# Low parts of x and of two weight groups summed by TensorE and copied out by ScalarE, in a gated linear attention with a feed-forward block

## The chip, the cores and the metric

The kernel runs on one core of a Trainium2 chip. The metric is the device time of one execution in microseconds. The kernel before took 530.58, 530.69 and 531.53 us in three runs; the median is 530.69 us.

In what follows PE is TensorE, DVE is VectorE, ACT is ScalarE, POOL is GpSimd and SP is the engine that only issues the transfers (DMA).

## The reference

A gated linear attention over 4 batches, 8 heads, 768 tokens and 48 elements a head feeds a two-layer feed-forward block:

```python
for t in range(S):
    state = alpha[:, :, t, :, None] * state + np.einsum('bhd,bhe->bhde', k[:, :, t], v[:, :, t])
    y[:, :, t] = np.einsum('bhd,bhde->bhe', q[:, :, t], state)
x = np.ascontiguousarray(y.transpose(0, 2, 1, 3)).reshape(B * S, H * D)   # 3072 x 384
h = x @ w_in                       # 384 x 2048
g = np.maximum(0.01 * h, h)
out = (g @ w_out).astype(np.float32)
```

q, k, v and alpha are float32. Both weight matrices are float32 values times a float64 scalar, so they arrive as float64, as pairs of 32-bit words, and the kernel takes the words apart itself.

## The kernel before, in words

**Precision.** The feed-forward products are done in fp32r, the faster and shorter form of float32 on PE. To keep float32's precision each operand is held as a high part (the value rounded to fp32r) and a low part (the value minus the high part, rounded too), and each product is the sum of three: high by high, high by low and low by high. The low parts are what the change is about. For x (the attention's output) they are made in `outputs`: ACT copies the sum y out of PSUM as the high part (L418), and DVE subtracts that from y into the low part (L419). For the weights they are made in `converting`, once for each of the 16 groups f of 128 hidden elements: ACT scales the upper words (L245), DVE builds a float32 `bits` from them (L248, L251), ACT rounds it to the high part (L254), DVE takes a power of two from it (L258), subtracts the high part (L260), scales the lower words by that power into `pw` (L262), and adds the two into the low part (L265).

**Attention.** A unit is 128 tokens of one batch, all 8 heads; there are 24, and three make a block of 384 tokens for the feed-forward part. For the first nine units (`u < AHEAD`) alpha, q and k are loaded token by token and transposed by PE (L280); for the others DVE transposes them. DVE makes the running product of alpha (L314) and a reversed one (L320) and scales q and k with them (L339, L347). PE then computes the scores of even heads from rows 0 to 47 and of odd heads from rows 64 to 111 of its array, into two PSUM tiles (L356), ACT copies them out (L366), POOL masks them (L367), PE transposes the scaled k back (L380), multiplies the old state by q (L395, from the fifth unit on), adds scores by v (L401) and computes the update of the state (L412). ACT sums absolute values of the two running products for a range check (L332).

**Feed-forward.** `ffn_in` runs nine matmuls of 384 columns for one block and one group f (L493), then ACT, DVE, ACT and DVE in turn make the activated high part `gh` (L496, L499, L501) and low part `gl` (L505); `ffn_out` runs nine matmuls into the three output tiles (L520), three steps later. Blocks 0 and 1 go together, group by group, while the weights are still being converted; the other six follow one by one with the attention of units 9 to 23 woven in.

**What sets the order.** The program is written in one order and a scheduler that estimates times orders the instructions of each engine anew, so a change of a few instructions can move others. Each engine then runs its own list strictly in that order. The conversions of groups 0, 1 and 2 are started while the attention of units 6 to 8 is done; those of later groups are held between the steps of blocks 0 and 1 by explicit lists (`put`).

**PSUM.** There are eight banks: two for `ph` (the feed-forward's first product), and three each of two kinds, `a` and `b`, that the attention takes in turn, eight of them a unit. The sum y of a unit lies in a bank of kind b for the first eight units and of kind a for the ninth.

**SP's queue.** All loads go through SP in one order: alpha, q, k and v of the first nine units, then the weight groups. v has three places, so v of unit u+3 is asked for once the outputs of unit u are done.

Of the kernel before, what the change touches and what calls it, by code (L numbers as in the profile page):

```python
# [9 lines left out]
F32 = mybir.dt.float32  # L10
F32R = mybir.dt.float32r
I32 = mybir.dt.int32
U32 = mybir.dt.uint32
I64 = mybir.dt.int64
AF = mybir.ActivationFunctionType
ALU = mybir.AluOpType
# [6 lines left out]
def gated_linear_attn_ffn(ctx, tc, q, k, v, alpha, w_in, w_out, out):  # L23
    nc = tc.nc
    B, H, S, D = q.shape
    NT, DM = out.shape
    DF = w_in.shape[1]
    P = 128
# [7 lines left out]
    BR = HB + D  # L36
# [12 lines left out]
    ps_h = fast.enter_context(tc.tile_pool(name="ps_h", bufs=2, space=bass.MemoryType.PSUM))  # L49
# [7 lines left out]
    PITCH = RUN + GAP  # L57
    AHEAD = 3 * UPB
    LAG = 3
    SOON, EARLY = 2, 3  # L60
    LEAD = 8
    SL = 8 * UPB
# [10 lines left out]
    def pieces(name, dtype, *shapes):  # L73

        sizes = [math.prod(shape) for shape in shapes]
        whole = cst.tile([P, sum(sizes)], dtype, name=name)
        parts = []
        for n, shape in enumerate(shapes):
            part = whole[:, sum(sizes[:n]):sum(sizes[:n + 1])]
            axes = "abc"[:len(shape)]  # L80
            if len(shape) > 1:
                part = part.rearrange(f"p ({' '.join(axes)}) -> p {' '.join(axes)}", **dict(zip(axes, shape)))
            parts.append(part)
        return parts
# [4 lines left out]
    state, vals_sb, rest = rest[:B], rest[B:B + NV], rest[B + NV:]  # L89
    loads_sb = [[rest.pop(0) for _ in range(n)] for n in NL]  # L90

    spare = pieces("spare", F32, *[(NP * PITCH,)] * 3)
    x_sb, = pieces("large", F32R, (3 * (NG + 1), 2, TB))

    w_sb = {}
# [8 lines left out]
    made = {}  # L104
# [75 lines left out]

    keep_warm(6)
    make_identity(nc, ident)
    nc.gpsimd.memset(mask, 1.0)
    nc.gpsimd.affine_select(
        out=mask, in_=mask, compare_op=ALU.is_ge, fill=0.0, base=0,
# [31 lines left out]
    def put(ordered, eng, op, *args):  # L217

        if not ordered:
            return op(*args)  # L220
        line = lines[eng]
        with tc.issue_after(line[-1].ins) if line else nullcontext():
            line.append(op(*args))
        return line[-1]

    def converting(f, ordered=False):

        if f >= NF:
            return
        raw = jobs.pop(f)  # L230
        w_sb[f] = cst.tile([P, 2, 2 * DM], F32R, name=f"w{f}")
        hi, lo = w_sb[f][:, HIGH, :], w_sb[f][:, LOW, :]
        if not f64:
            val = raw[:, :, 0:P].bitcast(F32)
            hi, lo = (t.rearrange("p (g f) -> p g f", f=P) for t in (hi, lo))
            nc.scalar.copy(hi, val)
            made["w", f] = nc.vector.tensor_tensor(lo, val, hi.bitcast(F32), ALU.subtract)
            return
        words = raw.rearrange("p g (f w) -> p (g f) w", w=2)
        top, low = words[:, :, 1], words[:, :, 0]  # L240
        bits = cvp.tile([P, 2 * DM], I32, name="bits", bufs=NBITS)
        val = bits.bitcast(F32)

        with nullcontext() if lines["ACT"] else behind(*AFTER.get(f, ("hi", f - 1))):
            put(ordered, "ACT", lambda: nc.scalar.mul(top.bitcast(F32), top.bitcast(F32), 2.0 ** -112))  # L245
        yield
        with nullcontext() if lines["ACT"] else behind("w", f - 1):
            put(ordered, "DVE", lambda: nc.vector.tensor_scalar(  # L248
                bits, top, 3, 0x7FFFFFF8, ALU.logical_shift_left, ALU.bitwise_and))
        yield  # L250
        put(ordered, "DVE", lambda: nc.vector.scalar_tensor_tensor(  # L251
            bits, top, -0x80000000, bits, ALU.bitwise_and, ALU.bitwise_or))
        yield
        made["hi", f] = put(ordered, "ACT", lambda: nc.scalar.copy(hi, val))  # L254
        yield
        pw = cvp.tile([P, 2 * DM], I32, name="pw", bufs=NPW)
        rest = pw.bitcast(F32)
        put(ordered, "DVE", lambda: nc.vector.tensor_scalar(pw, bits, -0x800000, None, ALU.bitwise_and))  # L258
        yield
        put(ordered, "DVE", lambda: nc.vector.tensor_tensor(val, val, hi.bitcast(F32), ALU.subtract))  # L260
        yield
        put(ordered, "DVE", lambda: nc.vector.scalar_tensor_tensor(  # L262
            rest, low.bitcast(U32), 2.0 ** -52, rest, ALU.mult, ALU.mult))
        yield
        made["w", f] = put(ordered, "DVE", lambda: nc.vector.tensor_tensor(lo, rest, val, ALU.add))  # L265
# [119 lines left out]
    def outputs(u):  # L385
        tb, b = units[u]
        i, j = divmod(u, UPB)
        pe, qs, ktok = live[u][:3]
        V, W = vals_sb[u % NV], state[b]
        at = i % 3 * (NG + 1)  # L390
        y = banks4()

        if tb:
            for p in range(NP):
                nc.tensor.matmul(  # L395
                    y[0:BR, p, :], W[0:BR, p, :], qs[0:BR, p, :], start=p == 0, stop=False, skip_group_check=True
                )
        for p in range(NP):
            for s, lo, m in ((0, 0, D if tb else HB), (1, HB, D)):
                c = (2 * p + s) * D  # L400
                nc.tensor.matmul(  # L401
                    y[lo:lo + m, p, :], V[:, c:c + m], masked[u][s][:, p, :],
                    start=not tb and p == 0, stop=p == NP - 1, skip_group_check=True,
                )
        del masked[u]
        kv = None
        if tb < NC - 1:
            kv = bank()[:, 0:NP * D].rearrange("d (p e) -> d p e", p=NP)
            for p in range(NP):
                for s, lo, m in ((0, 0, HB), (1, HB, D)):  # L410
                    h = 2 * p + s
                    made["kv", u] = nc.tensor.matmul(  # L412
                        kv[lo:lo + m, p, :], ktok[:, p, lo:lo + m], V[:, h * D:(h + 1) * D], start=True, stop=True
                    )
        load_values(u + NV)
        live[u] = pe, kv
        xh, xl = (x_sb[0:BR, at:at + NP, n, j * C:(j + 1) * C] for n in (0, 1))
        made["xh", u] = nc.scalar.copy(xh, y[0:BR])  # L418
        made["x", u] = nc.vector.tensor_tensor(xl, y[0:BR], xh.bitcast(F32), ALU.subtract)  # L419

    def next_state(u):
        tb, b = units[u]
# [61 lines left out]
    def ffn_in(i, f, steps=None):  # L484
# [14 lines left out]
        put(ordered, "DVE", lambda: nc.vector.tensor_tensor(t, ph, t, ALU.max))  # L499
        gh = ffp.tile([P, TB], F32R, name="gh", bufs=LAG + 1)  # L500
        put(ordered, "ACT", lambda: nc.scalar.copy(gh, t))  # L501
        for step in second:
            next(step, None)
        gl = ffp.tile([P, TB], F32R, name="gl", bufs=LAG + 1)
        made["gl", i, f] = put(ordered, "DVE", lambda: nc.vector.tensor_tensor(gl, t, gh.bitcast(F32), ALU.subtract))  # L505
# [48 lines left out]
    for n, _ in enumerate(st):  # L554
        if n == 2:
            load_values(NV - 1)
        while LOADS and LOADS[0][0] in made:
            key, f, part = LOADS.pop(0)
# [3 lines left out]
        u = AHEAD - EARLY + converted  # L562
# [4 lines left out]
        if n in STARTS:  # L567
            i, f = items[len(gs)][:2]
# [8 lines left out]
    for n in range(len(items) + LAG):  # L577
        slices = 0
        if n < len(items):
            i, f, slices, _ = items[n]  # L580
# [27 lines left out]
        for half in range(2):  # L608
# [5 lines left out]
            if half == 0 and n >= LAG:  # L614
                i, f, _, tag = items[n - LAG]
# [130 lines left out]
```

## Time and profile before

| | |
|---|---|
| median of 3 runs | 530.69 us |
| span of the profiled execution | 530.9 us |
| PE busy | 518.5 us (98%), 3778 matmul records |
| weight loads of PE busy | 500.0 us (94%) |
| DVE busy | 379.0 us (71%) |
| ACT busy | 230.7 us (43%) |
| POOL busy | 62.6 us (12%) |
| DMA | 46.64 MB |

The page shows no time around the span; the profiled execution's own time is taken as its span of 530.9 us, which lies within the three runs' 530.58 to 531.53.

Busy shares are means over unlike stages. The first 50 us or so are the attention of the first seven units, with all engines at work and the transfer engines full; then come two units more with the first feed-forward products, and from about 70 us on the feed-forward products alone, up to about 160 us. After that the rest of the attention and the feed-forward part run side by side. A float32 matmul shows as two records of PE, an fp32r matmul or a transpose as one.

### The profile page before, as it was taken

How to read it: one execution, taken by the hardware profiler on the slowest of the kernel's cores; microseconds unless marked ns; L12 is line 12 of the kernel's file. 1: busy time of each engine (PE TensorE's matmuls, PEld its weight loads, DVE VectorE, ACT ScalarE, POOL GpSimd, SP SyncE). 2: the span in 40 equal slices, each digit the busy share in tenths (PEclk: the TensorE clock that was granted, in tenths of full speed). 3: DMA queues.
4: the chain of work that ended last, by engine and by line, in shares of the span. 5: the costliest groups of instructions: out<-in, count | busy, mean ns of one | idle time of the engine just before them, and what ended most of it. 6: DMA issues, size and time to landing. Idle time of an engine off the chain costs nothing.

```text
span 530.9 us, 9962 instructions
## 1 busy us (share of the span) xinstructions
PE 518.5 (98%) x3778; PEld 500.0 (94%) x3778; DVE 379.0 (71%) x695; ACT 230.7 (43%) x489; POOL 62.6 (12%) x143
## 2 busy tenths in 40 slices
PE   8997999999999999999999999999999999999995
PEld 7886999999999999999999999999999999999995
DVE  6998899999999997777577586585786534333331
ACT  2764855555534444444334444345344444333331
POOL 4554500000000111100101101101010000000000
PEclk9998999999999999999999999999999999999998
DMA  9999975545726533552251431433201000101001
GB/s 144 168 175 170 229 172 133 131 122 141 170 45 184 127 84 81 102 134 49 60 111 30 112 83 44 92 74 86 54 15 25 31 16 1 23 1 44 1 0 51
DMA packets 92982, 46.64 MB, mean 88 GB/s; under 512 B 57856, under 2 KB 90112, under 8 KB 92928
## 3 DMA queue, kind: packets, MB, share of 16 engines
q1 hardware_dynamic: 92928, 45.93, 39.5%
q8 instruction: 32, 0.52, 0.4%
q14 instruction: 22, 0.18, 0.1%
HBM read 38.83 MB, written 4.72 MB: 82 GB/s over the span
## 4 chain that ended last, share of the span: by engine, by line
PE 87%; DVE 7%; DMA 4%; issue 1%; SPq 0%; DVEq 0%; ACT 0%
PE ph L493 35%; PE b L520 32%; PE a L356 4%; PE a L401 3%; PE a L520 3%; DMA small<-in_v_dram 3%; PE a L395 3%; PE a L412 2%; PE b L401 1%; PE a L380 1%; PE b L280 1%; DMA small<-in_alpha_dram 1%; DVE pw L262 1%; DVE gl L505 1%; DVE t L499 1%
## 5 line engine op out<-in xcount | busy, mean ns | idle before, releaser
L493 PE MATMUL ph<-large,w 128*128 128x384 f32 x1152 | 226.6, 338 | 0.5 <-DVE t L499 0.5
L493 PEld LDWEIGHTS ph<-large,w 128*128 128x128 f32 x1152 | 200.1, 188 | 2.8 <-DVE t L499 1.1
L520 PE MATMUL b<-w,gh 128*128 128x384 f32 x672 | 168.9, 340 | 0.0
L499 DVE TENSOR_TENSOR t<-ph,t 128x384 f32<-128x384 f32 x128 | 70.7, 553 | 79.1 <-ACT t L496 78.9
L520 PEld LDWEIGHTS b<-w,gh 128*128 128x128 f32 x672 | 119.4, 188 | 2.1 <-issue 0.4
L496 ACT ACTIVATE t<-ph 128x384 f32<-128x384 f32 x128 | 62.5, 489 | 128.2 <-PE ph L493 128.2
L501 ACT CAST gh<-t 128x384 fp32r<-128x384 f32 x128 | 65.7, 513 | 119.6 <-DVE t L499 119.6
L520 PE MATMUL b<-w,gl 128*128 128x384 f32 x336 | 107.4, 335 | 0.0
L505 DVE TENSOR_TENSOR gl<-t,gh 128x384 fp32r<-128x384 f32 x128 | 70.9, 554 | 34.3 <-ACT gh L501 34.2
L520 PEld LDWEIGHTS b<-w,gl 128*128 128x128 f32 x336 | 62.6, 188 | 0.0
L367 POOL TENSOR_SCALAR_AFFINE_SELECT sm<-sm 128x512 f32<-128x512 f32 x33 | 23.1, 712 | 207.8 <-ACT sm L366 207.8
L356 PEld LDWEIGHTS a<-qs,ks 48*128 48x128 f32 x312 | 24.1, 188 | 5.1 <-issue 4.2
L356 PE MATMUL a<-qs,ks 48*128 48x128 f32 x312 | 28.7, 285 | 0.0
L289 DVE STREAM_TRANSPOSE ks<-small 128x512 f32<-128x512 f32 x15 | 16.7, 1123 | 14.6 <-PE a L380 14.6
L324 POOL COPY pe<-pc 128x4 f32<-128x4 f32 x24 | 4.8, 202 | 163.7 <-DVE pc L314 163.7
L373 POOL TENSOR_TENSOR small<-us,pe 48x192 f32<-48x192 f32 x40 | 22.4, 560 | 1.5
L314 DVE TENSOR_TENSOR_SCAN pc<-e,small 128x128 f32<-128x128 f32 x60 | 20.4, 401 | 0.0
L366 ACT COPY sm<-a 128x512 f32<-128x512 f32 x24 | 14.0, 583 | 14.0 <-PE b L356 12.9
L520 PE MATMUL a<-w,gh 128*128 128x384 f32 x96 | 19.6, 337 | 0.0
L320 DVE TENSOR_TENSOR_SCAN rc<-e,small 128x511 f32<-128x511 f32 x15 | 19.1, 1276 | 0.2
L401 PE MATMUL a<-sm,small 128*48 128x128 f32 x256 | 17.7, 277 | 0.0
L254 ACT CAST w<-bits 128x768 fp32r<-128x768 f32 x16 | 13.4, 838 | 8.4 <-DVE bits L251 7.8
(92 smaller groups left out, 554.4 us busy)
## 6 DMA issues: line engine op xcount, KB each, us to landing
raw<-in_moe_w_out_dram SPq DMA_DIRECT2D x16, 384.0 KB, 3.8
small<-in_v_dram SPq DMA_DIRECT2D x24, 192.0 KB, 3.7
raw<-in_moe_w_in_dram SPq DMA_DIRECT2D x32, 144.0 KB, 4.0
out_dram<-o SPq DMA_DIRECT2D x24, 192.0 KB, 2.0
small<-in_alpha_dram SPq DMA_DIRECT2D x32, 96.0 KB, 2.3
small<-in_q_dram SPq DMA_DIRECT2D x30, 96.0 KB, 2.4
small<-in_k_dram SPq DMA_DIRECT2D x30, 96.0 KB, 2.2
small<-in_alpha_dram SPq DMA_DIRECT2D x30, 80.0 KB, 2.4
```

Of the source, the lines that this page charges most:

```text
L314: nc.vector.tensor_tensor_scan(pc[:, p, :], aT[:, p, :], ones.broadcast_to([P, C]), 1.0, ALU.mult, ALU.mult)
L320: nc.vector.tensor_tensor_scan(flat[2][:, NP * C - 2::-1], flat[0][:, NP * C - 1:0:-1], flat[1][:, NP * C - 2::-1], last, ALU.mult, ALU.add)
L356: nc.tensor.matmul(ss[s][:, p, :], ks[lo:lo + D, p, :], qs[lo:lo + D, p, :], start=True, stop=True)
L367: made["mask", u] = nc.gpsimd.affine_select(out=sm[s], in_=sm[s], compare_op=ALU.is_ge, fill=0.0, base=0, pattern=[[0, NP], [1, C]], chann ...
L373: nc.gpsimd.tensor_tensor(*scalings.pop(0))
L401: nc.tensor.matmul(y[lo:lo + m, p, :], V[:, c:c + m], masked[u][s][:, p, :], start=not tb and p == 0, stop=p == NP - 1, skip_group_check=True,
L493: nc.tensor.matmul(ph, w_in_of(f, wn, g), xt[:, g, :], start=n == 0, stop=n == 3 * NG - 1)
L496: put(ordered, "ACT", lambda: nc.scalar.mul(t, ph, 0.01))
L499: put(ordered, "DVE", lambda: nc.vector.tensor_tensor(t, ph, t, ALU.max))
L501: put(ordered, "ACT", lambda: nc.scalar.copy(gh, t))
L505: made["gl", i, f] = put(ordered, "DVE", lambda: nc.vector.tensor_tensor(gl, t, gh.bitcast(F32), ALU.subtract))
L520: product = nc.tensor.matmul(po[j], gt[:, js], w_out_of(f, wn), start=f == 0 and n == 0, stop=f == NF - 1 and n == 2)
```

## The change

For the first nine units the low part of x is no longer subtracted by DVE. PE adds the product of a negative identity (`minus`, made once by POOL) and the high part to the sum y where it lies in PSUM, which leaves y minus the high part there, and ACT copies that out. For weight groups 0 and 1 (`f < SUMS`) the last subtraction and the last addition on DVE are left out. PE sums identity by value, negative identity by high part and identity by scaled lower words in a PSUM tile of kind `ph`, for each half of 384 columns, and ACT copies the two sums out.

```diff
+    SUMS = 2
...
+    minus, = pieces("minus", F32R, (P,))
     x_sb, = pieces("large", F32R, (3 * (NG + 1), 2, TB))
...
     make_identity(nc, ident)
+    nc.gpsimd.tensor_scalar(minus, ident, -1.0, None, ALU.mult)
     nc.gpsimd.memset(mask, 1.0)
...
         put(ordered, "DVE", lambda: nc.vector.tensor_scalar(pw, bits, -0x800000, None, ALU.bitwise_and))
         yield
+        if f < SUMS:
+            nc.vector.scalar_tensor_tensor(rest, low.bitcast(U32), 2.0 ** -52, rest, ALU.mult, ALU.mult)
+            for cs in (slice(0, DM), slice(DM, 2 * DM)):
+                ps = ps_h.tile([P, 512], F32, name="ph")[:, 0:DM]
+                nc.tensor.matmul(ps, ident, val[:, cs], start=True, stop=False)
+                nc.tensor.matmul(ps, minus, hi[:, cs], start=False, stop=False)
+                nc.tensor.matmul(ps, ident, rest[:, cs], start=False, stop=True)
+                made["w", f] = nc.scalar.copy(lo[:, cs], ps)
+            return
         put(ordered, "DVE", lambda: nc.vector.tensor_tensor(val, val, hi.bitcast(F32), ALU.subtract))
...
         made["xh", u] = nc.scalar.copy(xh, y[0:BR])
-        made["x", u] = nc.vector.tensor_tensor(xl, y[0:BR], xh.bitcast(F32), ALU.subtract)
+        if u < AHEAD:
+            nc.tensor.matmul(y[0:BR], minus[0:BR, 0:BR], xh, start=False, stop=True, skip_group_check=True)
+            made["x", u] = nc.scalar.copy(xl, y[0:BR])
+        else:
+            made["x", u] = nc.vector.tensor_tensor(xl, y[0:BR], xh.bitcast(F32), ALU.subtract)
```

The new lines move the old ones by up to 16: L280 becomes L292, L356 L368, L366 L378, L380 L392, L395 L407, L401 L413, L412 L424, L418 L430, L332 L344. The new matmuls are L267, L268 and L269 (weights) and L432 (x); the new copies are L270 and L433.

The scheduler's order differs in the first 75 us or so; from the third weight group on, PE's list is the same as before. Three places:

PE, third unit (number 2), before, from its scores to its outputs. `a` and `b` are PSUM banks, `qs` and `ks` the scaled q and k, `ktok` (in later rows) the transposed k; `small` holds the loads and the identity.

```order
L356 MATMUL a_356<-qs_303,ks_311 128x128
L356 MATMUL b_357<-qs_303,ks_311 128x128
L356 MATMUL a_356<-qs_303,ks_311 128x128
L356 MATMUL b_357<-qs_303,ks_311 128x128
...
L380 MATMUL a_375<-small_73,ks_311 128x112 x4
L280 MATMUL a_392<-small_73 128x128 x4
L280 MATMUL b_384<-small_73 128x128 x4
L401 MATMUL b_400<-sm_366,small_73 64x128
```

The same place now; `b_316` is y of the unit before, `minus_75` the negative identity.

```order
L368 MATMUL a_360<-qs_306,ks_314 128x128 x4
L392 MATMUL a_379<-small_73,ks_314 128x112 x4
L368 MATMUL b_361<-qs_306,ks_314 128x128 x4
L292 MATMUL a_396<-small_73 128x128 x2
L432 MATMUL b_316<-large_76,minus_75 112x512
L292 MATMUL a_396<-small_73 128x128 x2
```

The eight score matmuls, which went to a and b in turn, are now four for a, then the transposes of k, then four for b. The same is so in units 4 and 6; in units 0, 1, 3, 5 and 7 they are in turn as before, and in unit 8 too, but for four of the sums that stand behind the first two. The sum for the unit before stands among the next transposes.

PE, seventh unit (number 6), where the sums for weight group 0 now stand (`ph_683` and `ph_688` are the two halves, `b_693` is y of unit 5). Before, L395 followed the transposes here directly.

```order
L368 MATMUL b_753<-qs_665,ks_672 128x128 x4
L432 MATMUL b_693<-large_76,minus_75 112x512
L292 MATMUL a_786<-small_73 128x128 x2
L267 MATMUL ph_683<-bits_675,small_73 128x384
L267 MATMUL ph_688<-bits_675,small_73 128x384
L268 MATMUL ph_683<-w0_674,minus_75 128x384
L268 MATMUL ph_688<-w0_674,minus_75 128x384
L424 MATMUL a_806<-small_73,ktok_775 64x48
...
L269 MATMUL ph_683<-pw_680,small_73 128x384
L269 MATMUL ph_688<-pw_680,small_73 128x384
L292 MATMUL b_779<-small_73 128x128 x4
L407 MATMUL b_793<-qs_665,small_73 112x128 x4
```

The update of the state (L424) moved ahead of the outputs (L407, L413), between the parts of the sums.

SP, around the seventh load of v (for unit 6), before:

```order
L139 DMA small_73<-in_q_dram 128x8x48
L449 DMA large_75<-large_75 16x3x768
L139 DMA spare_74<-in_alpha_dram 128x8x48
L449 DMA large_75<-large_75 16x3x768
L158 DMA small_73<-in_v_dram 128x8x48
L213 DMA raw_512<-in_moe_w_out_dram 128x384
```

And now:

```order
L141 DMA small_73<-in_q_dram 128x8x48
L465 DMA large_76<-large_76 16x3x768
L160 DMA small_73<-in_v_dram 128x8x48
L141 DMA spare_74<-in_alpha_dram 128x8x48
L216 DMA raw_518<-in_moe_w_out_dram 128x384
```

This load of v moved ahead of one load of alpha and of the second half of the first block's gather (`large` to `large`), which now comes after the second weight group.

## The prediction, on record before the change was run

> **What bounds the kernel now.** I read the page's busy shares first, then a table of stretches, then each engine's instructions in order of time through the stretch that the change touches. The shares are no answer by themselves:
>
> ```profile
> PE 518.5 (98%) x3778; PEld 500.0 (94%) x3778; DVE 379.0 (71%) x695; ACT 230.7 (43%) x489; POOL 62.6 (12%) x143
> ```
>
> The table by stretches has, for each: its length, the busy time of PE, of PE's weight loads, DVE, ACT and POOL, PE's granted clock, the share of the transfer engines and GB/s.
>
> ```profile
> 10.00:20.00 10.00, 9.93 (x130) 8.29 (x130) 9.71 (x23) 6.58 (x17) 4.41 (x11) 1.00 1.18 166
> 20.00:30.00 10.00, 9.67 (x132) 7.96 (x130) 9.44 (x21) 7.23 (x19) 6.29 (x15) 1.00 1.00 162
> 30.00:40.00 10.00, 9.88 (x122) 8.75 (x117) 9.05 (x20) 6.36 (x16) 5.21 (x13) 1.00 1.03 188
> 40.00:50.00 10.00, 6.55 (x78) 5.25 (x77) 9.52 (x18) 5.31 (x12) 6.08 (x8) 0.99 1.26 186
> 50.00:60.00 10.00, 10.00 (x119) 9.27 (x121) 8.47 (x17) 5.95 (x13) 3.22 (x6) 0.84 0.97 179
> 80.00:90.00 10.00, 10.00 (x59) 9.81 (x58) 10.00 (x18) 4.78 (x9) 0.00 (x0) 1.00 0.42 103
> ```
>
> From 10 to 50 us PE and DVE are both nearly full, so either might set the pace. What decides is who waits for whom. The scores (L356) need DVE's `qs`; the row of PE shows when they start, the row of DVE when `qs` was ready:
>
> ```profile
> 18.56 0.68 DVE L339 TENSOR_TENSOR qs<-b,pc 128x512 f32<-128x512 f32 x1
> ...
> 20.44 0.37 PE L356 MATMUL a<-qs,ks 48*128 48x128 f32 x1
> ```
>
> `qs` is done at 18.56 + 0.68 = 19.24, and PE comes to it 1.2 us later. Twice in this stretch it is DVE that waits for PE's transposes:
>
> ```profile
> 29.30 1.37 DVE L314 TENSOR_TENSOR_SCAN pc<-b,small 128x128 f32<-128x128 f32 x4 [0.20 <-PE b L280]
> ...
> 34.76 1.37 DVE L314 TENSOR_TENSOR_SCAN pc<-b,small 128x128 f32<-128x128 f32 x4 [0.53 <-PE b L280]
> ```
>
> So PE sets the pace, with one hole, in its rows between 44 and 53 us:
>
> ```profile
> 44.88 0.66 PE L280 MATMUL b<-small 128*128 128x128 f32 x4 [0.53 <-DVE rc L320]
> ...
> 46.56 0.63 PE L280 MATMUL b<-small,spare 128*128 128x128 f32 x4
> ...
> 49.98 0.42 PE L401 MATMUL b<-sm,small 128*48 128x128 f32 x1 [2.79 <-DMA small<-in_v_dram]
> ...
> 52.85 0.51 PE L356 MATMUL a<-qs,ks 48*128 48x128 f32 x1
> ```
>
> PE waits 2.79 us for v of unit 6, and after that its clock is 0.84 in the mean of the next ten microseconds. From 53 us on I find no idle time of PE up to the last block (the stretches of 50 and 80 us show it 10.00 busy of 10, and the rows of 81.26 and 82.86 below follow each other without a gap): whatever is added to PE there or before, beyond what this hole takes in, reaches the end.
>
> **The change part by part.** *Sums for x.* Nine matmuls of 512 columns in fp32r (L432). The nearest row is L493, 384 columns of the same type:
>
> ```profile
> 182.15 1.56 PE ph L493 x9
> ```
>
> That is 1.56 / 9 = 0.173 us each, so 0.173 × 512/384 = 0.231 at 512. Each stands between float32 transposes, and a change of shape and type costs PE a little: where the trace enters fp32r work from float32 work I find 0.08 us above the natural distance between starts; the nearest quoted row is the first score record, 0.37 against 0.27 for those that follow, 0.10. I take 0.231 + 0.084 = 0.315, nine times 2.8 us. Bounds: 9 × 0.231 = 2.1 with no entry, and 9 × 0.43 = 3.9 with twice 0.10.
>
> *Scores no longer in turn.* Today a score record of `a` and one of `b` start within 0.01 us of each other, since they use different rows of the array:
>
> ```profile
> 20.65 0.27 PE L356 MATMUL a<-qs,ks 48*128 48x128 f32 x1
> 20.66 0.27 PE L356 MATMUL b<-qs,ks 48*128 48x128 f32 x1
> 20.77 0.27 PE L356 MATMUL a<-qs,ks 48*128 48x128 f32 x1
> 20.77 0.27 PE L356 MATMUL b<-qs,ks 48*128 48x128 f32 x1
> ```
>
> A pair each 0.11 us, eight pairs a unit. Units 2, 4 and 6 now run four matmuls (eight records) of `a`, the transposes, and eight records of `b`: sixteen times 0.11 in place of eight, 8 × 0.107 to 0.11 = 0.87 us more. Three units: 2.6 us. Bounds: 0, if records of one row group are started as closely when the other is idle, and 3.3 with 0.2 for the shape changes of each.
>
> *Sums for two weight groups.* Each group has four float32 matmuls of 384 columns (L267, L269) and two in fp32r (L268). The nearest float32 row is L395, whose eight records are four matmuls of 128 columns:
>
> ```profile
> 39.05 0.88 PE b L395 x8
> ```
>
> 0.88 / 4 = 0.22 for 128 columns, 0.66 for 384. Four of these and two of 0.173 are 2.99 us a group, 6.0 for both; bounds 5.8 (0.107 a record, the closest spacing of score records) and 6.6 (0.1 for each of six changes of type). The trace shows float32 as two records of twice an fp32r record's length, four lengths in all: 0.66 against 0.173 is 3.8.
>
> [...]
>
> *Added to PE*: 2.8 + 2.6 + 6.0 = 11.4 us (bounds 7.9 to 13.8).
>
> *What the hole takes in.* v of unit 6 is asked for at 41.45 and lands at 49.84, after an alpha load and a gather half on SP's queue (the first three rows are SP's, the last is of the chain of waits):
>
> ```profile
> 40.08 0.55 SPq L139 DMA_DIRECT2D spare<-in_alpha_dram  x1
> 40.68 0.68 SPq L449 DMA_DIRECT2D large<-large  x1
> 41.45 0.54 SPq L158 DMA_DIRECT2D small<-in_v_dram  x1
> ...
> 41.45 8.39 DMA small<-in_v_dram
> ```
>
> In the change its issue moves ahead of those two, by about 1.3 us in the queue. It needs a place of v to come free at the outputs of unit 3, which PE reaches later by what is added to units 0 to 3 (three or four sums at 0.315 and one split, about 2 us), so I expect the landing between 49 and 51. PE comes to its first user later by the sums of units 0 to 5 (1.9), three splits (2.6) and group 0's first four matmuls and more (2 to 3): about 7 us of work after 46.56 + 0.6 = 47.2, less 0.8 of small idle times, so near 53. The wait is gone with 2 us to spare, and with it the slow clock: the rows above have 52.85 - 49.98 = 2.87 us from the first output to the next scores, where the unit before took
>
> ```profile
> 34.58 0.31 PE L401 MATMUL b<-sm,small 128*48 128x128 f32 x1
> ...
> 36.15 0.37 PE L356 MATMUL a<-qs,ks 48*128 48x128 f32 x1
> ```
>
> 1.57, 1.3 more; with the first score record at 0.51 for 0.37 that is 1.4. PE idles 10 - 6.55 = 3.45 in 40 to 50, and 0.3 in 20 to 30, on an earlier load of v. Together 3.45 + 1.4 + 0.3 = 5.15 us come back (bounds 3.3, the 2.79 and 0.53 alone, to 5.9, with the idle 0.7 that the stretches from 10 to 40 show beside).
>
> *DVE's relief.* It loses nine L419, and L260 and L265 twice:
>
> ```profile
> L419 DVE TENSOR_TENSOR large<-b,large 112x512 fp32r<-112x512 f32 x8 | 5.4, 673 | 0.8 <-ACT large L418 0.8
> L260 DVE TENSOR_TENSOR bits<-bits,w 128x768 f32<-128x768 f32 x9 | 9.0, 999 | 0.0
> L265 DVE TENSOR_TENSOR w<-pw,bits 128x768 fp32r<-128x768 f32 x9 | 8.6, 954 | 0.0
> ```
>
> 9 × 0.673 + 2 × (0.999 + 0.954) = 10.0 us. I cost it at nothing, since PE is late and not DVE. The one place where it may count is the stretch of steady feed-forward, where both are full:
>
> ```profile
> 81.26 1.60 PE ph L493 x9
> 82.86 1.58 PE a L520 x9
> ...
> 87.58 1.62 PE ph L493 x9
> ```
>
> 36 matmuls take 87.58 - 81.26 = 6.32 us, against 4 × 1.56 = 6.24 at PE's own rate: 0.08 a group, at most 0.9 us over the eleven groups to 150 us, and I count none of it. ACT's added copies (nine near 0.585, four near 0.515, 7.3 us) go to an engine that is half idle there; their price is only their place in the queue, which is a rival below. The one instruction on POOL is nothing beside its 4 to 6 us busy of 10.
>
> *Sum*: 11.4 - 5.15 = +6.2 on the profiled 530.9, so 537.1; that execution is 0.2 over the median, so **536.9 us**. Its own range, from the bounds: 7.9 - 5.9 = +2 to 13.8 - 3.3 = +10.5, 533 to 541.
>
> **The rivals.** *No change, about 531.* PE's busy time hides slack that the sums fill. For it: weight loads of PE are busy only 8.29 + 7.96 + 8.75 + 5.25 = 30.25 of the 40 us from 10 to 50, 9.75 us free, and with 1.4 of slow clock that is 11.2, nearly the 11.4 added: 530.9 + 0.2, 531. Against it: the score pairs' loads run side by side and the rows of PE follow each other at a constant distance, as in the rows of 20.65 to 20.77. [...] The wait of DVE for PE at 34.76 speaks against it. Chance 0.11.
>
> *Faster, about 526.* DVE, 95% busy, paces the first 50 us through a chain I have read wrongly, and 10 us less work on it pulls in all that follows. What it can win is capped by PE's idle time and slow clock, since PE has no gap after 53: 530.9 - 4.9 = 526, and it needs the sums to lie inside PE waits that the trace doesn't name. Against it: DVE's waits at 29.30 and 34.76. Chance 0.11.
>
> *Slower still, about 542.* The bank of y comes free later. Before, DVE's L419 frees it, in unit 1 at 22.31 + 0.67 = 22.98:
>
> ```profile
> 20.55 0.58 ACT L418 CAST large<-b 112x512 fp32r<-112x512 f32 x1 [0.44 <-PE b L401]
> ...
> 22.31 0.67 DVE L419 TENSOR_TENSOR large<-b,large 112x512 fp32r<-112x512 f32 x1
> ...
> 23.69 0.64 ACT L332 ACTIVATE rc<-rc 128x512 f32<-128x512 f32 x1
> ```
>
> Now ACT's second copy stands behind the next unit's score copies and sums of L332 in its queue, which ended at 24.33, so the bank can come 1.35 us later; there are three b banks and four uses a unit, and PE strictly in order waits with everything behind. Half of 1.35 in each of eight units is 5.4 above the forecast: 542. It decides if the copy ends after the next use of that bank is due. For it: PE is full, each wait counts. Against it: the sum itself stands early among the next transposes, and PE's own work per unit grows by more than 0.3. Chance 0.15.
>
> That the change doesn't do what it says can be left out: nine L419 and two of L260 and L265 are gone from DVE's list.
>
> **How the numbers follow.** Forecast 0.63, no change 0.11, faster 0.11, slower still 0.15. Such a measurement tells about 0.2% from no change, 1.1 us. Slower by more: the forecast less a little for its lower end, the last rival, and some of the no-change case that lies just beyond: 0.78; within: 0.10; faster: 0.12. The range leaves out the faster case and the top half of the last rival: 530.5 to 542.
>
> **What would show it.** No PE wait for v near 47 to 50 and a clock of 1.0 there; scores of units 2, 4, 6 at one record each 0.11 us; records of L267 and L269 at 0.33 spacing; the steady row of 81.26 about 6 us later, with period 6.3 unchanged. A b bank's wait on ACT's L433 ahead of L292 or L413 would speak for the last rival. If the steady row stands where it stood or earlier, the reading that PE sets the pace was wrong.

## The result, and the profile after

The changed kernel takes 539.15 us (median of four, 538.75 to 539.27); the kernel before, on the same chip, 531.11 us (530.58 to 532.03). The ratio is 1.015, interval 1.0135 to 1.0164: slower by about 8 us. Forecast were 536.9 us, in a range of 530.5 to 542, with a chance of 0.78 for slower.

The page of the changed kernel shows PE with 10 us more busy time and DVE with 9 us less:

```profile
PE 528.9 (98%) x3807; PEld 507.7 (94%) x3807; DVE 370.0 (69%) x682; ACT 238.1 (44%) x502; POOL 59.5 (11%) x144
```

The table by stretches (length, busy time of PE, weight loads, DVE, ACT, POOL; granted clock; share of the transfer engines; GB/s), for the changed kernel:

```profile
10.00:20.00 10.00, 9.80 (x131) 8.13 (x130) 8.69 (x19) 6.92 (x18) 4.43 (x11) 1.00 1.30 163
20.00:30.00 10.00, 10.00 (x102) 8.08 (x101) 7.81 (x17) 6.36 (x16) 4.73 (x12) 1.00 1.10 168
30.00:40.00 10.00, 10.00 (x117) 8.28 (x116) 6.78 (x16) 5.89 (x16) 4.73 (x11) 1.00 0.97 177
40.00:50.00 10.00, 10.00 (x99) 8.31 (x95) 8.86 (x18) 8.72 (x20) 4.96 (x10) 1.00 1.28 202
50.00:60.00 10.00, 9.58 (x88) 7.11 (x86) 6.34 (x14) 5.65 (x13) 3.61 (x8) 1.00 1.05 179
```

Against the same rows of before: the 6.55 of PE in 40 to 50 us is now 10.00, the clock of 0.84 in 50 to 60 is 1.00, and DVE has fallen from between 8.5 and 9.7 to between 6.3 and 8.9. The hole is full and its slow clock gone, as forecast; the 0.42 us that PE still idles in 50 to 60 us are a wait of L267 for DVE's `bits` in unit 7. PE's rows show what fills the hole. First unit 2, where `a` and `b` scores no longer start in pairs; then the stretch around the sums for weight group 0:

```profile
20.38 1.16 PE L368 MATMUL a<-qs,ks 48*128 48x128 f32 x8
21.47 0.60 PE L392 MATMUL a<-small,ks 112*128 112x112 f32 x4
22.00 1.16 PE L368 MATMUL b<-qs,ks 48*128 48x128 f32 x8
...
48.17 0.49 PE L432 MATMUL b<-large,minus 112*112 112x512 f32 x1
48.50 0.38 PE L292 MATMUL a<-small 128*128 128x128 f32 x2
48.73 1.45 PE L267 MATMUL ph<-bits,small 128*128 128x384 f32 x4
49.72 0.81 PE L268 MATMUL ph<-w,minus 128*128 128x384 f32 x2
50.46 0.67 PE L424 MATMUL a<-small,ktok 128*64 128x48 f32 x16
51.05 1.56 PE L269 MATMUL ph<-pw,small 128*128 128x384 f32 x4
```

Within each of the two pieces a row follows the last without idle time. In the chain of waits the row of steady feed-forward that stood at 81.26 now stands at

```profile
88.35 1.56 PE ph L509 x9
```

7.1 us later; its period has gone from 6.32 us to 6.26 (the next one is at 94.61).

The views of the cores give the span and the mean clock of a profile. Below are before, the changed kernel, and a second profile of before, taken beside the experiments (`before_again`):

```profile
core 0: 530.9 us, clock 0.994
```

```profile
core 0: 537.5 us, clock 0.999
```

```profile
core 0: 529.3 us, clock 0.997
```

The time of an execution is longer than its span, by 1.7 to 1.9 us in the runs here: 537.5 and 539.21 for the changed kernel, 529.3 and 530.99 for the second profile of before, 528.9 and 530.63 for another execution of it; 1.7 us in these three. So the first profile of before, with its span of 530.9, is an execution of about 532.6 us, some 1.5 to 2 us over the median. This is where the forecast went wrong, as shown below.

### The profile page after: what moved, and what is told of

Same layout as the page of the kernel before. It is cut to its first block, busy times and chain, and to the rows that moved or that the text cites. A ratio compares the mean times of both kernels' runs of the same rounds, so it can differ in the third digit from the quotient of the medians.

```text
span 537.5 us, 10018 instructions
## 1 busy us (share of the span) xinstructions
PE 528.9 (98%) x3807; PEld 507.7 (94%) x3807; DVE 370.0 (69%) x682; ACT 238.1 (44%) x502; POOL 59.5 (11%) x144
## 2 busy tenths in 40 slices
DMA packets 92982, 46.64 MB, mean 87 GB/s; under 512 B 57856, under 2 KB 90112, under 8 KB 92928
## 4 chain that ended last, share of the span: by engine, by line
PE 97%; DVE 1%; DMA 1%; issue 0%; ACT 0%
PE ph L509 38%; PE b L536 33%; PE a L536 5%; PE a L368 5%; PE a L413 3%; PE a L407 3%; PE a L424 2%; PE b L413 2%; PE a L392 2%; PE b L292 1%; DMA large<-large 1%; PE b L368 1%; PE ph L181 1%; PE a L292 1%; PE ph L267 1%; PE b L407 1%
## 5 line engine op out<-in xcount | busy, mean ns | idle before, releaser
L379 POOL TENSOR_SCALAR_AFFINE_SELECT sm<-sm 128x512 f32<-128x512 f32 x33 | 20.6, 634 | 203.9 <-ACT sm L378 203.9
L368 PEld LDWEIGHTS a<-qs,ks 48*128 48x128 f32 x312 | 23.9, 187 | 5.3 <-issue 4.5
L368 PE MATMUL a<-qs,ks 48*128 48x128 f32 x312 | 28.7, 285 | 0.2 <-DVE ks L359 0.2
L385 POOL TENSOR_TENSOR small<-us,pe 48x192 f32<-48x192 f32 x40 | 20.5, 512 | 1.5
L378 ACT COPY sm<-a 128x512 f32<-128x512 f32 x24 | 14.0, 583 | 14.7 <-PE b L368 11.6
L332 DVE TENSOR_TENSOR_SCAN rc<-e,small 128x511 f32<-128x511 f32 x15 | 19.1, 1271 | 0.2
L413 PE MATMUL a<-sm,small 128*48 128x128 f32 x256 | 17.3, 277 | 0.0
```

Source lines behind the costliest of these rows:

```text
L368: nc.tensor.matmul(ss[s][:, p, :], ks[lo:lo + D, p, :], qs[lo:lo + D, p, :], start=True, stop=True)
L379: made["mask", u] = nc.gpsimd.affine_select(out=sm[s], in_=sm[s], compare_op=ALU.is_ge, fill=0.0, base=0, pattern=[[0, NP], [1, C]], chann ...
L385: nc.gpsimd.tensor_tensor(*scalings.pop(0))
L413: nc.tensor.matmul(y[lo:lo + m, p, :], V[:, c:c + m], masked[u][s][:, p, :], start=not tb and p == 0, stop=p == NP - 1, skip_group_check=True,
```

## The experiments

Where PE's time is compared, it is summed from the distances between the starts of PE's records, by line, from the first record to the 73rd of the first feed-forward product (L493). This is the table for the changed kernel against the second profile of before:

```
                                       before   changed   difference
scores L356                             9.84     13.27      +3.43
sums for x (new)                        0.00      2.77      +2.77
sums for two weight groups (new)        0.00      6.43      +6.43
transposes L280                        17.00     14.54      -2.46
update of state L412                    6.03      5.11      -0.92
outputs L395, L401                     14.25     14.89      +0.64
first product L493                     13.32     12.72      -0.59
other                                  20.47     20.04      -0.43
start of the 73rd record               82.47     91.32      +8.85
start of the last record of PE        523.27    530.73      +7.46
```

A wait counts in the line that runs ahead of it, so the -2.46 of the transposes is mostly the waits that are gone. The spans of these two profiles differ by 8.2 us; 7.46 of them are there at the start of PE's last record, and 0.75 lie behind it (see the last section).

**The two parts apart.** First only the sums for x, with `SUMS = 0`.

```diff
-    SUMS = 2
+    SUMS = 0
```

> Only the sums for x; the two weight groups are summed by DVE as before. Units 2, 4 and 6 have their scores split as in the change. My theory (PE sets the pace, DVE's relief is worth nothing by itself): PE gets 2.8 us of sums and 3.3 us of split scores; of these about 5 us lie ahead of the wait for v of unit 6 and fill it (3.45 us and 1.4 us of slow clock come back), and the wait of 0.5 us at 163 us goes too. So the steady feed-forward row starts 1 to 1.5 us later than before and the time is 531 to 533 us. Rival 'DVE paces the first 50 us': 526 us, since DVE is relieved of 6 us. Rival 'the bank of y is held': PE waits on ACT's second copy ahead of the next users of a b bank, 535 us or more.

Measured: 534.22 us, ratio 1.0066 (1.0049 to 1.0084), 1.2 us above the range that was expected. The split scores cost 3.23 us of PE in it and the sums 2.68 us, and the hole was filled; but now PE waits for DVE's `qs` in units 7 and 8 (its list of waits, with microseconds in all, times, longest), and the wait of 0.4 us for DVE in the feed-forward part, which was to go, is still there:

```profile
PE b L368 <- DVE qs L351: 1.0, 1, 1.0
PE a L368 <- DVE qs L351: 0.6, 1, 0.6
```

Then only the sums for the weight groups.

```diff
-        if u < AHEAD:
+        if u < 0:
             nc.tensor.matmul(y[0:BR], minus[0:BR, 0:BR], xh, start=False, stop=True, skip_group_check=True)
```

> Only the sums for weight groups 0 and 1; x's low parts are subtracted by DVE as before, and all scores are in turn again. My theory: PE gets 6.4 us of sums; PE still comes early to v of unit 6, so of the 3.45 us wait only what the first sums of group 0 fill (2 to 3 us, if they stand ahead of the outputs of unit 6) comes back. Steady row 3 to 5 us later than before, time 534 to 536 us. Rival 'PE has slack that its busy time hides': 531 us.

Measured: 534.62 us, ratio 1.0073 (1.0055 to 1.009), as expected. The profiled execution is the slowest of the five, at 538.29 us; in it the sums took 7.5 us of PE, some of it at half clock (0.83 in the mean of 50 to 60 us), and a wait of 1.9 us for v of unit 6 stayed. The two parts, +3.6 and +4.0 us in the medians, add up to about the change's 8.

**The split scores.** They weren't asked for by the change. PE's rows show them split in `x_sums_alone` and in turn in `weight_sums_alone`, so the split comes with the sums for x; why the scheduler makes it isn't shown. An order of issue for the scores, and for the transposes of k behind them, puts them back in turn.

```diff
-                nc.tensor.matmul(ss[s][:, p, :], ks[lo:lo + D, p, :], qs[lo:lo + D, p, :], start=True, stop=True)
+                with behind("score", u):
+                    made["score", u] = nc.tensor.matmul(
+                        ss[s][:, p, :], ks[lo:lo + D, p, :], qs[lo:lo + D, p, :], start=True, stop=True)
```

> The change, with the sixteen score matmuls of each unit kept in turn between a and b by an order of issue, so that units 2, 4 and 6 aren't split. My theory: the split costs 3.3 us of PE in the change (sixteen records one by one in place of eight pairs), and the b bank is free when PE comes to it, so 536 us, 3 us under the change. Rival 'the bank of y is held': the scheduler split the scores because the bank comes late; PE then waits up to 1 us in each of the three units for ACT's second copy, and the time stays at 538 to 539 us.

Measured: 533.76 us, ratio 1.0057 (1.0039 to 1.0076), where 536 was expected: 5.4 us under the change in the medians, 4.4 us in the spans of the two profiles (533.1 and 537.5), and 4.0 us at PE's last record. By line 3.24 us is the scores, and 0.66 us the `keep_warm` matmuls of the first 11 us, which the change leaves as they are: by the same distances they take 5.82 us in the first profile of before and 6.56 in the changed kernel's. As for the rival of the held bank: PE's list of waits in this kernel has none for ACT. Three rows of DVE name a copy of ACT as what came last,

```profile
25.49 1.36 DVE L326 TENSOR_TENSOR_SCAN pc<-b,small 128x128 f32<-128x128 f32 x4 [0.50 <-ACT large L433]
30.56 1.36 DVE L326 TENSOR_TENSOR_SCAN pc<-b,small 128x128 f32<-128x128 f32 x4 [0.51 <-ACT large L433]
36.33 1.37 DVE L326 TENSOR_TENSOR_SCAN pc<-b,small 128x128 f32<-128x128 f32 x4 [0.94 <-ACT large L433]
```

but they don't show a bank that is held by the new copy. The lines of this kernel stand three lower than in the changed kernel, so L433 is the copy of the high part here, which the kernel before makes too, and the new copy is L436. And the scan reads what PE's transposes wrote into `b`, which end 0.1 us ahead of it each time, at 24.73 + 0.66 = 25.39 for the first:

```profile
24.73 0.66 PE L292 MATMUL b<-small 128*128 128x128 f32 x4
```

On PE the price of the sums' order was the split; a price of the held bank doesn't show.

**DVE's relief alone.** The change with its 21 matmuls left out and all copies kept.

> The change with its 21 matmuls left out: DVE is relieved as in the change and ACT makes the same copies, but of y itself and of the scaled lower words, so the low parts of x for nine units and of two weight groups are not computed. It shows what DVE's relief alone is worth. My theory: nothing in the first 75 us, since PE is late and not DVE: the wait for v of unit 6 stays, 530 to 531 us (0.5 us less if the wait of the first feed-forward product for DVE at 163 us goes). Rival 'DVE paces the first 50 us': 526 us or less.

Measured: 530.41 us, ratio 0.9995 (0.9982 to 1.0008). Ten microseconds less work on DVE are worth nothing that can be measured. The scores are in turn in this kernel, though ACT makes the same copies from the same banks, so it is not these copies alone that split them. The hole of PE stays, as expected: v of unit 6 lands at 48.83, and POOL's `pe`, which the row names, comes 0.1 us behind it.

```profile
48.96 0.42 PE L409 MATMUL b<-sm,small 128*48 128x128 f32 x1 [2.32 <-POOL pe L332]
```

**More of the same work.** Two more matmuls behind each sum for x, on the kernel with scores in turn; `zero` is a matrix of zeros, made by POOL as `minus` is.

```diff
-            nc.tensor.matmul(y[0:BR], minus[0:BR, 0:BR], xh, start=False, stop=True, skip_group_check=True)
+            for m in (minus, zero, zero):
+                nc.tensor.matmul(y[0:BR], m[0:BR, 0:BR], xh, start=False, stop=m is zero, skip_group_check=True)
```

> The change with scores in turn, and with two more matmuls behind each sum for x that add zero times the high part (the result stays the same): 18 more matmuls of 512 columns on PE and nothing else. My theory (each us of PE reaches the end once the hole is filled): 18 times 0.231, so 4.2 us over the change with scores in turn, 533.8 + 4.2 = 538.0 us. Rival 'PE has slack that its busy time hides': under 1.5 us more, 534 to 535 us.

Measured: 539.68 us, ratio 1.0164 (1.0136 to 1.0192). The sums took 7.18 us in place of 2.77, 4.4 more, and PE's last record is 4.4 us later (531.11 and 526.69). The medians differ by 5.9 us, 1.7 more than expected, but they are of two sets of runs; the profiled spans differ by 4.8. PE's time reaches the end in full.

**The hole.** The second profile of before answers how much it is worth.

> The kernel before, unchanged, profiled once more. The span of the profile of before was 530.9 us at a mean clock of 0.994, while its other executions beside the first experiments had spans of 528.0 to 530.3 at clocks of 0.991 to 1.0. My theory: the slow clock of 50 to 53 us that I counted as recovered is a thing of some executions, and a second profile has a span of about 529 us with a clock near 1.0 in 50 to 60 us, but the same wait of about 3 us for v of unit 6. Rival: the hole always brings the slow clock, and the second profile looks like the first, 530.9 us and 0.84 in 50 to 60 us.

It came at 529.3 us. Its rows of the hole, and the granted clock in the first profile by the microsecond:

```profile
44.94 0.66 PE L280 MATMUL b<-small 128*128 128x128 f32 x4 [0.53 <-DVE rc L320]
48.14 0.28 PE L401 MATMUL b<-sm,small 128*48 128x128 f32 x1 [1.05 <-DMA small<-in_v_dram]
```

```profile
49.00:50.00 1.00, 0.02 (x2) 0.05 (x3) 1.00 (x3) 0.00 (x0) 0.31 (x1) 0.87 1.33 189
50.00:51.00 1.00, 1.00 (x16) 1.00 (x18) 0.82 (x3) 0.00 (x0) 0.05 (x1) 0.50 1.29 170
51.00:52.00 1.00, 1.00 (x16) 1.00 (x15) 0.44 (x2) 0.00 (x0) 0.14 (x1) 0.50 0.66 87
52.00:53.00 1.00, 1.00 (x11) 0.64 (x7) 0.79 (x1) 0.04 (x1) 0.00 (x0) 0.50 0.36 70
```

In the second profile the wait is 1.05 us in place of 2.79, where some 3 us were expected again, and the clock stays at 1.00, as expected. So neither the 1.7 us of longer wait nor the 1.4 us of slow clock is a thing of each execution.

**Can the hole be closed without sums?** First the weight loads were put behind the load of v.

```diff
-    LOADS = [(("v", 4), 0, 0), (("v", 5), 0, 1), (("v", 6), 1, None), (("g", 1), 2, None), (("v", 8), 3, None)]
+    LOADS = [(("v", 4), 0, 0), (("v", 6), 0, 1), (("v", 6), 1, None), (("g", 1), 2, None), (("v", 8), 3, None)]
```

> The kernel before, with the upper half of the first weight group's loads and all of the second asked for after v of unit 6, so that v comes some 5 us earlier. No sums. My theory (PE sets the pace but for this hole): the wait of 2.8 us goes and with it any slow clock after it, so 527 us, 3 to 4 us under before, and the times scatter less. Rival 'the hole is worth nothing, since DVE or the transfers are as late': another wait takes its place (PE for v of unit 7, or for DVE's rc or qs) and the time is 530 us.

Measured: 536.94 us, ratio 1.0109 (1.0081 to 1.0137), a miss on all counts. v of unit 6 was asked for at 41.10, hardly earlier than in the two profiles of before (41.45 and 41.04), and landed at 46.56 in place of 49.84 and 48.00. PE doesn't wait for it, but only since it stands still from 43.74 on for another reason: ACT's list has the first step of group 0's conversion (L245) ahead of the copies of the attention, and that step now waits for its weights, with everything behind it:

```profile
51.12 1.12 PE L280 MATMUL a<-small 128*128 128x128 f32 x4 [7.37 <-DVE us L432]
```

```profile
48.25 0.88 ACT L245 ACTIVATE raw<-raw 128x768 f32<-128x768 f32 x1 [7.64 <-DMA raw<-in_moe_w_in_dram]
49.16 0.56 DVE L248 TENSOR_SCALAR bits<-raw 128x768 int32<-128x768 int32 x1 [7.14 <-ACT raw L245]
```

So this run doesn't tell what an early v is worth. Then v alone was put ahead, of the gather of block 0 and of one load of alpha, with `with behind("v", 2 * UPB):` around both.

> The kernel before, without any sum, and with v of unit 6 asked for ahead of the gather of block 0 and of one load of alpha; the loads of the weights keep their places. It comes 2 us earlier than the 41.0 to 41.5 us of the two profiles of before. My theory: the wait for v of unit 6 (1.05 us in the second profile of before, 2.79 in the first) falls to under 0.8 us, and with the hole the half clock goes: 528.5 to 530 us, with less scatter and a mean clock of 0.998 or more in each execution. Rival 'the hole is worth nothing': a wait for DVE's rc or for alpha takes its place, 530.5 to 531.

Measured: 531.35 us, ratio 1.0002 (0.9992 to 1.0013). The rival held: the wait for v is gone, and at the same place PE waits for DVE's `qs`, which DVE makes behind its conversion of group 0 (first row PE's, second DVE's):

```profile
49.67 0.37 PE L357 MATMUL a<-qs,ks 48*128 48x128 f32 x1 [1.00 <-DVE qs L340]
```

```profile
47.76 1.25 DVE L263 SCALAR_TENSOR_TENSOR pw<-raw,pw 128x768 f32<-128x768 uint32 x1
48.94 0.68 DVE L340 TENSOR_TENSOR qs<-b,pc 128x512 f32<-128x512 f32 x1
```

So these two were changed over, by issuing the rest of that conversion behind ks of unit 7.

> The kernel before with v of unit 6 ahead, and with one more thing: the last steps of group 0's conversion are issued behind ks of unit 7, by which DVE makes qs of unit 7 ahead of the scaling into pw (1.25 us) and not behind it. Nothing else moves on DVE. My theory now: the hole of PE at 47 to 50 us has two locks, the load of v and DVE's late qs, since DVE converts group 0 there; with both opened PE's wait for qs (1.00 us at 49.67 with v ahead alone) goes, the steady feed-forward row comes 1 us earlier, and the time is about 1 us less, 530 us. Rival 'a third lock': another wait of the same length (for POOL's masks or for ACT's copies) stands there and the row stays.

Measured: 531.84 us, ratio 1.0012 (0.9999 to 1.0026). Again the rival held. `qs` is made 1.2 us earlier, and now it is the load of alpha, the one that had been put behind v, which comes last (from 54 to 64 us three more waits of 0.8 to 1.0 us follow, for ACT, DVE and POOL):

```profile
47.73 0.68 DVE L340 TENSOR_TENSOR qs<-b,pc 128x512 f32<-128x512 f32 x1
```

```profile
47.72 0.63 PE L281 MATMUL b<-small,spare 128*128 128x128 f32 x4 [1.09 <-DMA spare<-in_alpha_dram]
```

**Sums for x in turn, with and without the earlier v.**

> Only the sums for x, with the scores kept in turn: neither split nor weight sums. My theory: PE gets 2.8 us, of which 1.9 us (six sums) and the 0.5 us of the wait at 163 us come back, so at least as good as before: 529 to 531 us, and 3 us under the sums for x with split scores (534.2). Rival 'PE is not the pacer there, DVE's qs is late instead' (it was, by 0.6 and 1.0 us, with the scores split): 532 to 534 us.

Measured: 531.58 us, ratio 1.0015 (0.9997 to 1.0033), 2.6 us under the sums with split scores, and not to be told from before.

> The same order of loads together with the sums for x, scores in turn. My theory: with v early nothing is left for the sums to fill, so 9 sums of 0.31 us cost 2.8 less the 0.5 us that DVE's relief gives at 163 us: 2 us over the kernel with v ahead alone, 530.5 to 532 us. Rival 'DVE is the pacer at 40 to 50 us and its relief counts there': as fast as v ahead alone or faster.

Measured: 531.51 us, ratio 1.0013 (0.9998 to 1.0029), not to be told from `v_ahead`, so the 2 us that were expected aren't there, and what came is what the rival had said: as fast as `v_ahead` alone. In both kernels PE still has a hole; it waits for DVE's `rc`, which stands behind the same conversion. From the list of PE's waits in the first, and from PE's rows in the second:

```profile
PE b L410 <- DVE rc L332: 2.3, 1, 2.3
```

```profile
47.74 1.13 PE L411 MATMUL b<-qs,small 112*112 112x128 f32 x8 [2.29 <-DVE rc L333]
```

At that place it is DVE that is late, as the rival has it. Nine sums for x are therefore nearly free if the scores stay in turn (between 0.2 us less and 1.8 us more than before, by the interval of the first), and they win nothing either. That they are free because they fit in this hole is likely, but not shown apart from DVE's relief.

**The copy on DVE.** On the kernel with scores in turn:

```diff
-            made["x", u] = nc.scalar.copy(xl, y[0:BR])
+            made["x", u] = nc.vector.tensor_copy(xl, y[0:BR])
```

> The change with scores in turn (533.8 us), with the copy of x's low part made by DVE in place of ACT. My theory: neither ACT's place in the queue nor DVE's relief matters, since PE sets the pace: 533 to 535 us. Rival 'the bank of y is held by ACT's copy behind other work': 1 to 3 us faster, 531 to 533. Rival 'DVE paces': 9 copies of some 0.6 us on it, 3 us or more slower, 537.

Measured: 536.19 us, ratio 1.009 (1.0076 to 1.0105), 2.4 us more than with ACT's copy in the medians, 1.5 us at PE's last record. It lies between what was expected, and there is no gain from an earlier bank. DVE's copies take 6 us, and ahead of them DVE stands idle for 4.5 us more until PE has made the sums:

```profile
L436 DVE CAST large<-b 112x512 fp32r<-112x512 f32 x8 | 5.4, 673 | 4.5 <-PE b L435 4.5
```

Some 10 us of DVE's time thus cost 1.5 to 2.4 us. DVE isn't the pacer, but it has little to spare.

No version here beats the kernel before by more than can be measured.

## Why the prediction was right, and by what it missed

**What sets the pace.** "PE sets the pace, with one hole" held: `no_sums` shows DVE's relief at nothing, `x_sums_three_times` PE's time at its full price. The hole was misread, though. I named one wait, for v; the last experiments show that four things are due there within about two microseconds, v, DVE's `qs` and `rc` behind the conversion of group 0, and a load of alpha, and that opening one lock only shows the next.

**The terms added.** Sums for x: 2.8 forecast, 2.77 measured. Split scores: 2.6 forecast, 3.43 measured, a little over the upper bound of 3.3. About 3.24 of it are the three split units: each run of eight records of one kind takes 1.09 us (20.38 to 21.47), and the 0.2 us for two changes of shape that I had kept for the bound belong in the value. That `a` and `b` records start together since they use different rows agrees with these runs: sixteen of them in turn take as long as eight of one kind, 1.09 us (20.44 to 21.53 in unit 2 of before), while the float32 sums for weights, which use all rows, start one by one, 0.32 us apart, though they go to two banks. The other 0.19 are unit 8, whose scores are cut in two by sums for weights. Sums for weights: 6.0 forecast, 6.43 measured; sixteen float32 records at 0.323 and four of 0.173 make 5.86, and six starts of a new shape, 0.07 to 0.11 us each, the rest, which I had kept for the bound too. (The wait of 0.42 us for `bits` isn't in it.) Together 12.6 for 11.4.

**What the hole gives back.** The wait for v went and the clock was 1.00, as forecast; v was asked for at 40.18 against 41.45, 1.3 us earlier:

```profile
40.18 0.54 SPq L160 DMA_DIRECT2D small<-in_v_dram  x1
```

It landed at 45.19, 5.0 us later in place of 8.4, and not between 49 and 51 as forecast; PE came to it at 53.85, near the 53 of the forecast, so the wait would have been gone either way.

Against the first profile of before the table's sum would give 12.6 - 5.7 = 6.9 us back, against the second 12.6 - 7.5 = 5.1; 5.15 was forecast. The agreement with the second is partly luck, as the parts differ: the 1.4 us of clock and 1.7 us of the wait aren't in it, but other small waits before 70 us are, and 1.4 us that I hadn't counted, between the 73rd record and the 361st. I wrote that from 53 us on PE has no idle time. There was one, in this row of before,

```profile
163.57 1.15 PE L493 MATMUL ph<-large,w 128*128 128x384 f32 x5 [0.47 <-DVE t L499]
```

where DVE has just begun unit 9's attention beside the feed-forward steps. In the changed kernel PE comes there without a wait:

```profile
169.57 1.20 PE L509 MATMUL ph<-large,w 128*128 128x384 f32 x6
```

By the distances of starts this is 0.72 us, half of the 1.4; the rest lies in small pieces over the steady period (0.11 us at most at a place) and in the scores at 185 us (0.17).

**The step that failed** is the last one: "that execution is 0.2 over the median". For want of a time around the span I had set it to nothing, and put the profile's span of 530.9 beside the median time of 530.69. It is 1.7 to 1.9 us in the runs here, so the profiled execution was about 2 us over the median, and it was so for the very wait and slow clock that my sum took back: its 73rd record starts 1.8 us later than that of the second profile, and its last record still does. From time to time the forecast fell 2.2 us short of 539.15. From span to span it was 537.1, and the profile has 537.5, but that agreement is luck in part: 1.2 us more were added than forecast, 1.8 us more came back, and the stretch behind PE's last record, which the forecast took as unchanged, is 0.95 us longer.

**The rivals.** No change, on the ground of the weight loads' free share: refuted, since 18 matmuls more came at full price with weight loads busy for 7.7 to 8.7 of each 10 us from 10 to 60. Faster by DVE's relief: refuted by `no_sums`. The held bank: it is held longer (in unit 1's stretch of the changed kernel the copy ends at 24.24 + 0.60 = 24.84, where L419 of before ended at 22.98 and I had reckoned with 24.3 or later),

```profile
24.24 0.60 ACT L433 CAST large<-b 112x512 fp32r<-112x512 f32 x1
```

but PE's list of waits in the changed kernel has none for ACT. What the sums for x did cost beyond their own time was the order that the scheduler chose with them.

## What to carry to other kernels

Before a difference of 1% is forecast from one profile, ask whether that execution is a usual one: compare span with span, and find what lies between span and time (1.7 to 1.9 us here). A hole in the bounding engine is worth its length only if nothing else is due at the same place; look for the second and third arrival before counting it, and count its slow clock only as far as executions show it each time. And when work is moved to another engine in a kernel with a scheduler, the cost may be largest where the order changes: here the split of the scores, which no line of the change mentions, took more of PE (3.2 us) than the nine sums for x (2.8).

## What the runs showed of the hardware

In five of the fourteen profiles the granted clock fell to one half between 45 and 55 us, during a wait of PE or soon behind one, and came back later. In the first profile of before, by tenths of a microsecond, it is 1.00 up to 49.7 us, 0.74 in the tenth to 49.8, 0.50 up to 53.1, 0.70 in the next tenth and 1.00 again from 53.2 on: one step down and one step up. PE's last record ahead of the hole ended there at 47.2 us and the clock fell at 49.74 (a mean of 0.87 in the stretch from 49 to 50 is 0.74 us at 1.00 and the rest at 0.50). In `early_v`, where PE ended at 43.74, it fell at 46.78 by the same reckoning, and came back only at 57.0, 6 us after PE had begun to work again at 51.12:

```profile
46.00:47.00 1.00, 0.00 (x0) 0.00 (x0) 0.00 (x0) 0.00 (x0) 0.00 (x0) 0.89 0.42 131
47.00:48.00 1.00, 0.00 (x0) 0.00 (x0) 0.00 (x0) 0.00 (x0) 0.00 (x0) 0.50 0.42 91
...
56.00:57.00 1.00, 1.00 (x18) 1.00 (x19) 1.00 (x3) 0.00 (x0) 0.74 (x1) 0.50 0.94 148
57.00:58.00 1.00, 1.00 (x22) 0.81 (x20) 1.00 (x4) 0.00 (x0) 0.00 (x0) 0.99 0.99 203
```

In `no_sums` it fell at 47.32, 0.7 us after PE had ended at 46.64 behind two waits of 0.5 and 0.4 us, and came back at 57.56:

```profile
47.00:48.00 1.00, 0.00 (x0) 0.00 (x0) 1.00 (x4) 0.24 (x1) 0.60 (x2) 0.66 1.16 274
...
57.00:58.00 1.00, 1.00 (x7) 0.90 (x6) 0.00 (x0) 0.63 (x2) 0.77 (x2) 0.72 1.08 253
```

In `x_sums_in_turn` PE idled from 45.74 to 48.04, and the clock was one half from 47.32 to about 54.2 (0.79 in the mean of 50 to 60 us); in `v_ahead_x_sums` it idled as long, from 45.45 to 47.74, and the clock stayed at 1.00. In `weight_sums_alone` it fell only at 50.40, 1.4 us after PE's idle time from 47.11 to 49.02, and came back at 53.80 (0.60 in the mean of 50 to 52 us, 0.55 in 52 to 54).

So the fall came between 0.7 us into the idle time and 1.4 us behind its end, and the slow clock cost 1.4 us in one profile of before and nothing in the other. From the fall to the return it is 3.4 us in the first profile of before (back at 53.16, by the same reckoning from the 0.92 of its stretch from 53 to 54) and in `weight_sums_alone`, 6.9 us in `x_sums_in_turn`, and 10.2 us in `early_v` and `no_sums`. What sets the moment of the fall and the length isn't shown: `no_sums` was at one half three times as long as before, though PE was at work from 48.96 on in it and from 49.98 on in before.

The time from the start of PE's last record to the end of the span, with three stores of the output in it, was 5.8 and 6.0 us in the two profiles of before, 6.8 in the changed kernel's and 5.1 in that of `v_ahead`. The instructions there are the same in all. Most of the difference is how long the slowest of the three stores takes from issue to landing: 3.6 and 3.8 us, 4.2 and 3.0. In the five profiles of kernels that make sums for weights this stretch is 6.4 to 6.8 us, in the nine others 5.1 to 6.0; with one profile of each, why the stores differ stays open.
